# The opening of a fused recurrent-attention and expert kernel: who moves the first gate sums, who fills the head rows, and what stands ahead of the first units

## The chip, the cores and the metric

The kernel runs on one core of one Trainium2 chip. Its time is the device time of one execution in microseconds (us), the median of 3 runs. A row of the profile names five engines: PE (TensorE; PEld is its weight load), DVE (VectorE), ACT (ScalarE), POOL (GpSimd) and SP (SyncE). SP, ACT and POOL also issue transfers (DMA), which all share 16 DMA engines. A q behind an engine's name (SPq, ACTq) is its queue of issues.

## What is computed

An attention with exponential gates and a state, then a mixture of eight experts with the two best chosen for each token:

```python
batch, n_heads, seq, head_dim = (4, 8, 768, 40)
for t in range(S):
    m_new = np.maximum(f_gate[:, :, t] + m, i_gate[:, :, t])
    f_stab = np.exp(f_gate[:, :, t] + m - m_new)
    i_stab = np.exp(i_gate[:, :, t] - m_new)
    m = m_new
    C = f_stab[:, :, None, None] * C + i_stab[:, :, None, None] * np.einsum('bhd,bhe->bhde', vt, kt)
    n = f_stab[:, :, None] * n + i_stab[:, :, None] * kt
    h_tilde = np.einsum('bhde,bhe->bhd', C, qt)
    denom = np.maximum(np.abs(nq), 1.0)              # nq = n . q
    y[:, :, t] = o * h_tilde / denom                 # o = sigmoid(o_gate)
# x = y as 3072 tokens of 320
noisy_logits = x @ w_gate + np.log1p(np.exp(x @ w_noise)) * noise
# the two best of 8 experts; out += weight * (relu(x @ w1[e]) @ w2[e])
```

## The kernel before

The 768 steps of a sequence are cut into 12 chunks of 64, and two sequences are worked at a time (in the two halves of the partitions), so that the attention has 24 units. Unit u needs: its q and k (tile qk, four buffers, four loads: two of 32 partitions and two of 8), its k, v and output gate in rows (tile vk, four buffers, two loads), and a mask of 64 by 64 for every head, the exponential of a difference of gate sums. The masks come from PE: `e_part` multiplies LE by RE (98 rows) once for each sequence p, and ACT takes the exponential into W.

LE and RE exist twice, and each serves a group of two units: group 0 is units 0 and 1 (buffers le0, re0), group 1 is units 2 and 3 (le1, re1), group 2 is units 4 and 5 (le0, re0 again). They are put together of four pieces: constants copied by ACT (`operands`, L230), the head rows 64 to 95 of RE (`heads`, L237, 32 x 1024 for each p), and the gate sums of the group, which DVE works out in eight instructions (`gate_math`, L196, ending with L218) and which two small transfers then carry to other partitions (`gate_move`, L223: first le, then re). Before the masks of a group can be multiplied, all of these must be there.

Other work of the opening: `blank` clears qk where a load leaves gaps, and the 8-partition loads go on top of it; `keys` (L246, POOL: two memsets and two copies of a unit matrix from cs) prepares a vk buffer, which `k_part` (kd) and `c_part` read; `warm` runs dummy matmuls on PE. The third group's gate sums (256 to 383) are worked out by `gate_steps`, four instructions at a time.

The instructions of an engine run in the order in which the code is written. Order on PE at the start: 16 dummies, `s_part(0)` (scores), `WARM2` dummies, `e_part(0)`, `s_part(1)`, `e_part(1)`, then the loop over units. Pass i of the loop (L792) does `c_part(i)` (st, state), `o_part(i)` (o, output), the first half of the masks of unit i+2, later `s_part(i+2)`, then the other half of those masks. Behind the first half, ACT does the sigmoid of unit 0 in pass 0 (`sig_part`, L326 to L328), DVE normalises (`f_part`, L384 to L390), and POOL multiplies the two into xr (L391). In pass 0 POOL then issues `gate_move(2, (P, P))` (L840), the gate sums of group 2. The first half of unit 4's masks, in pass 2, reads them.

Transfers issued by SP and ACT raise one of eight counters, DMAHW0 to DMAHW7, taken in turn in the order of the code over both queues. A transfer that reuses a counter first waits until the transfer that had it before, eight places earlier, has landed; behind it in its queue everything waits too. POOL's transfers have eight counters of their own, DMASW0 to DMASW7.

After the attention come the routing (mostly within the loop) and eight experts of large matmuls.

Of the kernel before, what the change touches and what calls it, by code (L numbers as in the profile page):

```python
# [13 lines left out]
OP = mybir.AluOpType  # L14
# [4 lines left out]
L = 64  # L19
# [18 lines left out]
PAD = 544  # L38

STEP, SHARE = 0.19, 1.65  # L40
WARM, WARM2 = 16, 12
LEAD = 2
TURN = 6
OR1 = (0, 6, 1, 2, 3, 4, 5)
# [7 lines left out]
GC = 2  # L52
# [9 lines left out]
def build(ctx, tc, qk, vk, fi, noise, wgn, w1, w2, cst, ce, out):  # L62
    nc = tc.nc
    V, A, P, T, SP = nc.vector, nc.scalar, nc.gpsimd, nc.tensor, nc.sync
# [10 lines left out]
    cs = keep.tile([128, C_END], F32, name="cs")  # L75
# [78 lines left out]
    def load_unit(u, what="kv", q=None):  # L154
        pr, c = divmod(u, NCH)
        if "k" in what:
            for n in (slice(0, 32), slice(32, D)):
                for p in range(2):
                    (q or SP).dma_start(QK[u % 4][64 * p + n.start:64 * p + n.stop], qk[pr, c, p, n])
        if "v" in what:  # L160
            flat = VKS[u % 4].rearrange("p x c -> p (x c)")
            SP.dma_start(flat[0:64, 0:VW], vk[pr, c, 0])
            SP.dma_start(flat[64:128, 648:648 + VW], vk[pr, c, 1])
# [12 lines left out]
    def blank(i, q):  # L176
        q.memset(QK[i][32:64], 0.0)
        q.memset(QK[i][96:128], 0.0)
# [3 lines left out]
    V.memset(mt[:, 0:1], -1e30)  # L182
    blank(0, V)
    blank(1, P)
    V.memset(rmt[:, 0:256], 1.0)
    V.memset(rmt[:, 0:256].rearrange("p (c t) -> p c t", t=L)[:, :, 0], 0.0)
    load_unit(0, "k")
    SP.dma_start(cs[:, 0:128], cst[:, 0:128])
    SP.dma_start(fit[:, :, 128:384], fi[:, :, 128:384])
    load_unit(0, "v")  # L190

    def run(steps):
        for _ in steps:
            pass

    def gate_math(t0, t1):  # L196
        f, i = fit[:, 0, t0:t1], fit[:, 1, t0:t1]
        n = t1 - t0
        V.tensor_tensor_scan(mt[:, t0 + 1:t1 + 1], f, i, mt[:, t0:t0 + 1], OP.add, OP.max)
        yield  # L200
        gt = gts[t0 // 128 % 2][:, 0:n]
        V.tensor_add(gt, f, mt[:, t0:t1])
        yield
        V.tensor_sub(gt, gt, mt[:, t0 + 1:t1 + 1])
        if t0 == 0:
            V.memset(gt[:, 0:1], 0.0)
        yield
        ag = ags[t0 // 128 % 2][:, :, 0:n]
        V.tensor_tensor_scan(ag[:, 1, :], rmt[:, 0:n], gt, 0.0, OP.mult, OP.add)
        yield  # L210
        V.tensor_sub(ag[:, 0, :], i, mt[:, t0 + 1:t1 + 1])
        yield
        V.tensor_sub(ag[:, 0, :], ag[:, 0, :], ag[:, 1, :])
        yield

        V.tensor_copy(HL[:, :, t0:t1], ag)
        yield
        V.scalar_tensor_tensor(HL[:, :, t0:t1], HL[:, :, t0:t1].bitcast(F32), cet[0:64, E_SG:E_SG + 1], ag, op0=OP.mult, op1=OP.add)  # L218
        yield
# [3 lines left out]
    def gate_move(kk, q=(SP, SP)):  # L223
        pr, k = divmod(kk, GB)
        j = kk % 2
        src = HL[32 * pr:32 * pr + 32, :, k * GC * L:(k + 1) * GC * L].bitcast(F32)
        q[0].dma_start(LE[j][64:96, :, 64:128].bitcast(F32), src[:, 0].rearrange("r (c t) -> r c t", c=GC))
        q[1].dma_start(RE[j][96:98].bitcast(F32), src[:, 1])

    def operands(j, p, eng=None):  # L230
        if p is None:
            A.activation(LE[j][0:KE], cet[0:KE, None, E_L:E_L + 192].to_broadcast([KE, GC, 192]), AF.Copy)
        else:
            A.activation(RE[j][0:64, p].rearrange("r h (c t) -> r h c t", c=GC),
                         cet[0:64, None, None, 0:L].to_broadcast([64, H, GC, L]), AF.Copy)

    def heads(j, p, eng):  # L237
        o, i = RE[j][64:96, p], cet[64:96, E_H:E_H + H, None].to_broadcast([32, H, GC * L])
        x = cet[64:96, E_P + p:E_P + p + 1]
        if eng is A:  # L240
            A.activation(o, i, AF.Copy, scale=x)
        else:
            V.tensor_scalar(o, i, x, None, op0=OP.mult)


    def keys(i):  # L246
        P.memset(VK[i][1][32:64, 0:328], 0.0)
        P.memset(VK[i][0][96:128, 328:648], 0.0)
        P.tensor_copy(VK[i][0][64:104, 328:648].rearrange("p (h d) -> p h d", h=H), ident[64:104, None, 64:104].to_broadcast([40, H, D]))
        P.tensor_copy(VK[i][1][0:64, 328:648].rearrange("p (h d) -> p h d", h=H), ident[0:64, None, 0:D].to_broadcast([64, H, D]))  # L250

    operands(0, None, A)
    load_unit(1, "k", A)
    run(gate_math(0, GC * L))
    gate_move(0)
    operands(0, 0, A)
    operands(0, 1, A)
    heads(0, 0, A)
    heads(0, 1, A)
    load_unit(1, "v")  # L260
    blank(2, P)
    for i in range(2):
        keys(i)
    load_unit(2, "k")
    operands(1, None, A)
    operands(1, 0, A)
    run(gate_math(GC * L, 256))
    gate_move(1)
    heads(1, 0, V)
    gates2 = (s for t0 in (256, 384, 512, 640) for s in gate_math(t0, t0 + 128))  # L270

    def gate_steps(n):
        for _ in range(n):
            next(gates2, None)

    gate_steps(4)
    blank(3, P)
    for i in range(2, 4):
        keys(i)
    load_unit(2, "v")  # L280
    load_unit(3, "k")
    SP.dma_start(fit[:, :, 384:], fi[:, :, 384:])
# [61 lines left out]
    def whole(u):  # L344
        return u % NCH > 0

    def k_part(u):
        if u % NCH < NCH - 1:
            KD[u] = wk.tile([128, 2, H, D], F32, name="kd")
            V.tensor_mul(KD[u], VKS[u % 4][:, :, 328:648].rearrange("p x (h d) -> p x h d", h=H),  # L350
                         W[u][:, :, :, L - 1:L].to_broadcast([128, 2, H, D]))

    def p_part(u):
        PP[u] = wk.tile([128, 2, H, L], F32, name="p")
        if whole(u):
            V.tensor_mul(PP[u], SQ[u], W[u])
        else:
            for p in range(2):
                n = half[p]
                V.tensor_mul(PP[u][n, p], SQ[u][n, p], W[u][n, p])  # L360
# [336 lines left out]
    warm(WARM2)  # L697
    e_part(0, first=True)
    s_part(1)
    heads(1, 1, A)  # L700
    e_part(1, first=True)
    operands(1, 1, A)
    k_part(0)
    p_part(0)

    load_unit(3, "v")
    def route(i):
# [83 lines left out]
    i = 0  # L791
    while i < NU - LEAD:  # L792
        unit[0] = i
        spent[0] = 0.0
        while sent:
            SP.dma_start(*sent.pop())
        if 1 <= i and i + 3 < NU:
            load_unit(i + 3)
        if i:
            keep_rows(i - 1)  # L800
        if i % 2 == 0 and i and i // 2 + 2 < 2 * GB:
            gate_move(i // 2 + 2, (P, P) if i < XV else (SP, SP))

        if W1LD <= i < W1LD + 12 and i % 2 == 0:
            j = (i - W1LD) // 2
            piece_w1(0, 512 * (j // 3), j % 3)
        if i == W2AT:
            early_w2(0, 2)
        if i == 3:
            SP.dma_start(cs[:, C_TRI:], cst[:, C_TRI:])  # L810
        if i == 4:
            SP.dma_start(nzt, noise)
        if not begun and done[0] >= E0U[0]:
            decode(0, E0S[1] // 128)
            spent[0] += 0.6
            begun = 1
        if begun and late < len(tiles(0, 0)):
            gather(0, 0, tiles(0, 0)[late:late + 2])
            late += 2
            begun = 2  # L820
        if i == 6:
            constants()
            A.activation(tri, cs[:, C_TRI:C_TRI + 128], AF.Copy)
            A.activation(ones, cs[:, C_ONE:C_ONE + 128], AF.Copy)
            A.activation(iob, cs[:, C_N:C_N + 128], AF.Copy)
        k_part(i + 1)
        p_part(i + 1)
        fill(0.2, False)
        s_room(i + 2)
        c_part(i)  # L830
        o_room(i)
        o_part(i)
        e_part(i + LEAD, (0,))
        if i == 0:
            sig_part(0)
        f_part(i, lambda: fill(0.15, False))
        if i < 2:
            gate_steps(4)
        if i == 0:
            gate_move(2, (P, P))  # L840
        t = l_part(i)
        w = r_part(t)
        b = None if w else b_part(t)
        if i:
            t_part(i - 1)
            tc_part(i - 1)
        lc_part(i, t, w)
        bc_part(t, b)
        s_part(i + 2)
        act()  # L850
        if i:
            sig_part(i + 1)
        e_part(i + LEAD, (1,))
        if i == 0:
            sig_part(1)
        route(i)
        fill((SHARE if i < NU - 3 else 0.8) - spent[0])
        if W1AT <= i < W1AT + 12 and i % 2 == 0:
            next(pre1)
        act()  # L860
        if 0 < i < 7:
            gate_steps(4)
        if 6 <= i < 13:
            P.memset(XG[:, i - 6], 0.0)
        i += 1
# [352 lines left out]
    with tc.If(over > 0):  # L1218
        for i in range(NE):
            n = BLK - CAPS[i]  # L1220
            more = nc.values_load(flag[0:1, 2 + i:3 + i], min_val=0, max_val=16 * NTOK)
            with tc.If(more > 0):
# [4 lines left out]
                x = xf[0:n, 0:RW]  # L1227
# [12 lines left out]
        with tc.If(most > BLK):  # L1240
            V.memset(ec, 0.0)
            with tc.For_i(0, NE, 1) as e:
                weights(e)
                with tc.For_i(0, NCH, 1) as c:
# [8 lines left out]
                    for r in range(2):  # L1253
                        x = xf[:, DM * r:DM * r + DM]
# [93 lines left out]
```

## Time and profile before

| | us |
|---|---|
| median of 3 runs (lowest to highest) | 523.07 (521.63 to 526.06) |
| the profiled execution | 522.65 |
| its span, first to last instruction | 520.9 |
| PE busy in the span | 504.6 (97%) |
| DVE, ACT, POOL busy | 341.3, 248.7, 243.3 |
| first mask on PE begins | 12.20 |
| first half of unit 4's masks begins | 29.00 |

The profiled execution lies 0.42 us under the median, and its span 1.75 us under its own time. Matmuls are pipelined, so a busy PE isn't PE at its peak. The chain of waits is followed back from the last instruction: it names at each step what released the step. A wait for several things is put down to the one that came last by the profile.

### The profile page before, as it was taken

The page shows a single profiled execution, that of the slowest core. Times are in us where ns is not written, and L with a number is a line of the kernel's source. Part 1 is how long each engine was busy: PE and PEld are TensorE (multiplying, and loading weights), DVE is VectorE, ACT ScalarE, POOL GpSimd, SP SyncE. Part 2 cuts the span into 40 slices and gives each one's busy share as a digit, 9 for nine tenths or more (in the row PEclk, how much of TensorE's full clock was granted, in tenths as well). Part 3 has the DMA queues.
Part 4 walks back from the last instruction along what each step waited for, and adds up shares of the span by engine and source line. Part 5 has one row for each costly group of instructions (what it writes and reads, how often), then busy time and mean ns, then how long its engine had stood idle before and what let it go on. Part 6 is the DMA issues. An engine that isn't in the chain of part 4 may idle for free.

```text
span 520.9 us, 13365 instructions
## 1 busy us (share of the span) xinstructions
PE 504.6 (97%) x5130; PEld 473.3 (91%) x5130; DVE 341.3 (66%) x905; ACT 248.7 (48%) x594; POOL 243.3 (47%) x321
## 2 busy tenths in 40 slices
PE   8899999999999999999999999999999999999993
PEld 3788888888889988999999999999999999999993
DVE  6899998986997576763865484377548347546310
ACT  5788879978523255441542354054335325515300
POOL 7545686864543846055415614550562254151033
PEclk9799999999989999999999999999999999999998
DMA  5889999986655848079229516832951683272033
GB/s 153 201 217 243 246 242 248 223 235 207 216 195 165 202 57 213 5 163 234 68 53 274 112 28 139 229 91 48 263 99 51 138 221 88 60 169 26 2 40 41
DMA packets 48955, 76.89 MB, mean 148 GB/s; under 512 B 10645, under 2 KB 37980, under 8 KB 48884
## 3 DMA queue, kind: packets, MB, share of 16 engines
q1 hardware_dynamic: 35668, 52.19, 36.3%
q0 software_dynamic: 11616, 20.57, 20.7%
q10 hardware_dynamic: 1600, 3.21, 2.0%
q8 instruction: 42, 0.69, 0.6%
q14 instruction: 29, 0.24, 0.2%
HBM read 52.42 MB, written 17.40 MB: 134 GB/s over the span
## 4 chain that ended last, share of the span: by engine, by line
PE 66%; DMA 13%; DVE 11%; ACT 3%; issue 2%; POOL 2%; SPq 1%; POOLq 0%; DVEq 0%; ACTq 0%
PE s L981 16%; DMA y_out<-y,tok 9%; PE e L981 8%; PE o L1009 4%; PE o L1008 4%; PE o L1007 4%; PE st L1008 4%; PE st L1009 4%; PE st L1007 4%; PE o L379 4%; PE e L318 3%; PE s L342 2%; DVE hlo L993 2%; PE st L370 2%; DMA qk<-qk_in 2%
## 5 line engine op out<-in xcount | busy, mean ns | idle before, releaser
L1035 POOL DMA_INDIRECT y_out<-y,tok x53 | 87.2, 1645 | 184.8 <-DVE y L1025 182.0
L992 ACT ACTIVATE hh<-s 128x384 fp32r<-128x384 f32 (+3 forms) x91 | 42.6, 470 | 83.8 <-PE s L981 82.7
L981 PE MATMUL s<-xh,w1h 128*128 128x384 f32 (+6 forms) x273 | 76.8, 337 | 0.1
L750 POOL DMA_INDIRECT xg<-rows,tok x53 | 57.3, 1082 | 24.6 <-issue 15.5
L993 DVE SCALAR_TENSOR_TENSOR hlo<-s,hh 128x384 fp32r<-128x384 f32 (+3 forms) x91 | 47.6, 523 | 24.9 <-ACT hh L992 24.3
L981 PE MATMUL s<-xh,w1l 128*128 128x384 f32 (+6 forms) x273 | 61.7, 334 | 0.0
L1009 PE MATMUL o<-w2h,hlo 128*128 128x320 f32 x184 | 56.9, 309 | 0.7 <-DVE hlo L993 0.7
L1008 PE MATMUL o<-w2l,hh 128*128 128x320 f32 x184 | 56.8, 309 | 0.0
L1007 PE MATMUL o<-w2h,hh 128*128 128x320 f32 x184 | 56.3, 306 | 0.2 <-ACT hh L992 0.2
L1009 PE MATMUL st<-w2h,hlo 128*128 128x320 f32 x168 | 51.9, 309 | 0.0
L1008 PE MATMUL st<-w2l,hh 128*128 128x320 f32 x168 | 51.8, 308 | 0.0
L1007 PE MATMUL st<-w2h,hh 128*128 128x320 f32 x168 | 51.2, 305 | 0.0
L981 PEld LDWEIGHTS s<-xh,w1h 128*128 128x128 f32 x273 | 49.2, 188 | 1.5 <-ACT xh L782 0.4
L981 PEld LDWEIGHTS s<-xh,w1l 128*128 128x128 f32 x273 | 47.7, 188 | 1.1 <-DVE xh L784 0.2
L981 PE MATMUL s<-xl,w1h 128*128 128x384 f32 (+6 forms) x182 | 46.1, 334 | 0.3 <-DVE xl L783 0.3
L992 ACT ACTIVATE hh<-e 128x384 fp32r<-128x384 f32 (+3 forms) x45 | 21.3, 473 | 49.3 <-PE e L981 49.3
L981 PE MATMUL e<-xh,w1h 128*128 128x384 f32 (+6 forms) x135 | 38.6, 340 | 0.6 <-DVE hlo L993 0.3
L1025 DVE TENSOR_SCALAR y<-o,gw 128x320 f32<-128x320 f32 x22 | 12.1, 550 | 39.9 <-PE o L1009 39.9
L391 POOL TENSOR_TENSOR xr<-tm,vk 128x320 f32<-128x320 f32 x24 | 21.1, 879 | 34.7 <-DVE tm L390 13.6
L1025 DVE TENSOR_SCALAR y<-st,gw 128x320 f32<-128x320 f32 x20 | 11.0, 550 | 39.3 <-PE st L1009 39.3
L1009 PEld LDWEIGHTS o<-w2h,hlo 128*128 128x128 f32 x184 | 34.5, 188 | 0.9 <-DVE hlo L993 0.9
L1007 PEld LDWEIGHTS o<-w2h,hh 128*128 128x128 f32 x184 | 34.5, 188 | 0.6 <-ACT hh L992 0.4
(237 smaller groups left out, 1290.7 us busy)
## 6 DMA issues: line engine op xcount, KB each, us to landing
vk<-vk_in SPq DMA_DIRECT2D x48, 242.0 KB
raw<-w_in SPq DMA_DIRECT2D x6, 1280.0 KB
raw<-w_in SPq DMA_DIRECT2D x6, 1024.0 KB
qk<-qk_in SPq DMA_DIRECT2D x46, 128.0 KB
y_out<-zrow SPq DMA_DIRECT2D x15, 320.0 KB
raw<-w_in SPq DMA_DIRECT2D x16, 256.0 KB
rows<-xr POOLq DMA_DIRECT2D x23, 160.0 KB, 4.3
xt__2801<-xb SPq DMA_DIRECT2D x40, 72.0 KB
```

Of the source, the lines that this page charges most:

```text
L318: T.matmul(ps, LE[j][0:KE, c, 64 - 64 * p:192 - 64 * p], RE[j][0:KE, p, :, c * L:c * L + L], start=True, stop=True)
L379: T.matmul(OQ[u][half[p], h, :], PP[u][n, p, h, :], VK[u % 4][p][n, h * 41:h * 41 + 41], start=True, stop=True)
L391: P.tensor_mul(XR[u], tm.rearrange("p h d -> p (h d)"), SG[u % 4])
L750: P.indirect_dma_start(out=XG[0:rows_of(e, t), t], out_offset=None, in_=XD[0:n], in_offset=bass.IndirectOffsetOnAxis(ap=token(e, t), axis= ...
L981: T.matmul(ps[:, 0:n], l, r, start=i == 0, stop=i == len(ops) - 1)
L992: A.activation(hi, x, AF.Relu)
L993: V.scalar_tensor_tensor(lo, x, 0.0, hi.bitcast(F32), op0=OP.max, op1=OP.subtract)
L1007: T.matmul(ps, HH[:, j, c], W2H[:, j], start=j == 0, stop=False)
L1008: T.matmul(ps, HH[:, j, c], W2L[:, j], start=False, stop=False)
L1009: T.matmul(ps, HLO[:, j, c], W2H[:, j], start=False, stop=j == 7)
L1025: V.tensor_scalar(y[0:n], ps[0:n], GW[e][0:n, t:t + 1], None, op0=OP.mult)
L1035: st = P.indirect_dma_start(out=out, out_offset=bass.IndirectOffsetOnAxis(ap=token(e, t), axis=0), in_=y[0:n], in_offset=None, compute_op= ...
```

## The change

- The second set of dummies has 6 instead of 12.
- SP loads the unit matrix (cs) ahead of unit 0's q and k, and unit 1's q and k, which ACT issued, are now issued by SP behind unit 0's vk.
- The gate sums of group 0 are issued by ACT instead of SP.
- The head rows: (0,0) go from ACT to POOL, (0,1) from ACT to DVE, (1,0) from DVE to POOL, (1,1) from ACT to POOL.
- The first four instructions of the third group's gate arithmetic go from ahead of the first units' DVE work to behind `p_part(0)`.
- On POOL `blank(2)` is written earlier, and `keys(3)` goes from ahead of the loop into pass 0, between xr of unit 0 and `gate_move(2)`.

```diff
@@ -38,7 +38,7 @@
 PAD = 544
 
 STEP, SHARE = 0.19, 1.65
-WARM, WARM2 = 16, 12
+WARM, WARM2 = 16, 6
 LEAD = 2
 TURN = 6
 OR1 = (0, 6, 1, 2, 3, 4, 5)
@@ -182,12 +182,14 @@
     V.memset(mt[:, 0:1], -1e30)
     blank(0, V)
     blank(1, P)
+    blank(2, P)
     V.memset(rmt[:, 0:256], 1.0)
     V.memset(rmt[:, 0:256].rearrange("p (c t) -> p c t", t=L)[:, :, 0], 0.0)
+    SP.dma_start(cs[:, 0:128], cst[:, 0:128])
     load_unit(0, "k")
-    SP.dma_start(cs[:, 0:128], cst[:, 0:128])
     SP.dma_start(fit[:, :, 128:384], fi[:, :, 128:384])
     load_unit(0, "v")
+    load_unit(1, "k")
 
     def run(steps):
         for _ in steps:
@@ -240,7 +242,7 @@
         if eng is A:
             A.activation(o, i, AF.Copy, scale=x)
         else:
-            V.tensor_scalar(o, i, x, None, op0=OP.mult)
+            eng.tensor_scalar(o, i, x, None, op0=OP.mult)
 
 
     def keys(i):
@@ -250,33 +252,30 @@
         P.tensor_copy(VK[i][1][0:64, 328:648].rearrange("p (h d) -> p h d", h=H), ident[0:64, None, 0:D].to_broadcast([64, H, D]))
 
     operands(0, None, A)
-    load_unit(1, "k", A)
-    run(gate_math(0, GC * L))
-    gate_move(0)
     operands(0, 0, A)
     operands(0, 1, A)
-    heads(0, 0, A)
-    heads(0, 1, A)
+    heads(0, 0, P)
+    keys(0)
+    run(gate_math(0, GC * L))
+    gate_move(0, (A, A))
+    heads(0, 1, V)
     load_unit(1, "v")
-    blank(2, P)
-    for i in range(2):
-        keys(i)
+    keys(1)
     load_unit(2, "k")
     operands(1, None, A)
     operands(1, 0, A)
     run(gate_math(GC * L, 256))
     gate_move(1)
-    heads(1, 0, V)
+    heads(1, 0, P)
+    heads(1, 1, P)
     gates2 = (s for t0 in (256, 384, 512, 640) for s in gate_math(t0, t0 + 128))
 
     def gate_steps(n):
         for _ in range(n):
             next(gates2, None)
 
-    gate_steps(4)
     blank(3, P)
-    for i in range(2, 4):
-        keys(i)
+    keys(2)
     load_unit(2, "v")
     load_unit(3, "k")
     SP.dma_start(fit[:, :, 384:], fi[:, :, 384:])
@@ -697,11 +696,11 @@
     warm(WARM2)
     e_part(0, first=True)
     s_part(1)
-    heads(1, 1, A)
     e_part(1, first=True)
     operands(1, 1, A)
     k_part(0)
     p_part(0)
+    gate_steps(4)
 
     load_unit(3, "v")
     def route(i):
@@ -837,6 +836,7 @@
         if i < 2:
             gate_steps(4)
         if i == 0:
+            keys(3)
             gate_move(2, (P, P))
         t = l_part(i)
         w = r_part(t)
```

The built programs differ on each engine up to pass 0 alone; behind it the order is the same. Three places follow, with the waits of each row. In the names the number behind qk, vk, le and re is the buffer (unit 0 to 3 for qk and vk, group 0 or 1 for le and re); hl is the tile that holds the gate sums.

SP before, from unit 0's vk on:

```order
L162 DMA vk0_104<-vk_in 64x968 [waits DMAHW4_49]
L163 DMA vk0_104<-vk_in 64x968 [waits DMAHW5_49]
L227 DMA le0_94<-hl_96 32x2x64 [waits DMAHW6_49,DVE_49,Activation_49]
L228 DMA re0_92<-hl_96 2x16x128 [waits DMAHW7_49]
L162 DMA vk1_105<-vk_in 64x968 [waits DMAHW0_49]
L163 DMA vk1_105<-vk_in 64x968 [waits DMAHW1_49]
L159 DMA qk2_102<-qk_in 32x1024 [waits DMAHW2_49]
L159 DMA qk2_102<-qk_in 32x1024 [waits DMAHW3_49]
L159 DMA qk2_102<-qk_in 8x1024 [waits DMAHW4_49,Pool_49]
L159 DMA qk2_102<-qk_in 8x1024 [waits DMAHW5_49,Pool_49]
L227 DMA le1_95<-hl_96 32x2x64 [waits DMAHW6_49,DVE_49,Activation_49]
L228 DMA re1_93<-hl_96 2x16x128 [waits DMAHW7_49]
```

SP now, from behind unit 0's vk on:

```order
L159 DMA qk1_101<-qk_in 32x1024 [waits DMAHW4_49]
L159 DMA qk1_101<-qk_in 32x1024 [waits DMAHW5_49]
L159 DMA qk1_101<-qk_in 8x1024 [waits DMAHW6_49,Pool_49]
L159 DMA qk1_101<-qk_in 8x1024 [waits DMAHW7_49,Pool_49]
L162 DMA vk1_105<-vk_in 64x968 [waits DMAHW0_49]
L163 DMA vk1_105<-vk_in 64x968 [waits DMAHW1_49]
L159 DMA qk2_102<-qk_in 32x1024 [waits DMAHW2_49]
L159 DMA qk2_102<-qk_in 32x1024 [waits DMAHW3_49]
L159 DMA qk2_102<-qk_in 8x1024 [waits DMAHW4_49,Pool_49]
L159 DMA qk2_102<-qk_in 8x1024 [waits DMAHW5_49,Pool_49]
L229 DMA le1_95<-hl_96 32x2x64 [waits DMAHW6_49,DVE_49,Activation_49]
L230 DMA re1_93<-hl_96 2x16x128 [waits DMAHW7_49]
```

The two issues for le0 and re0 are gone from SP, and four for qk1 stand there. le0 and re0, now on ACT, take the counters DMAHW6 and DMAHW0, as PE's wait for the first mask shows; so qk1's third piece waits on SP for le0 to land, and vk1's first for re0. PE now, from the first mask on:

```order
L317 MATMUL e_260<-re0_92,le0_94 128x512 [waits DMAHW0_49,DMAHW6_49,Activation_49,Pool_49]
L317 MATMUL xt_205<-re0_92,le0_94 128x512 [waits DVE_49,Activation_49]
L338 MATMUL s_236<-qk1_101,cs_66 64x256 [waits DMAHW7_49,DMAHW5_49,DMAHW2_49]
L338 MATMUL s_236<-qk1_101,cs_66 64x256 [waits DMAHW6_49,DMAHW4_49]
L341 MATMUL s_236<-qk1_101 64x64 x8
L338 MATMUL s_236<-qk1_101,cs_66 64x256 x2
L341 MATMUL s_236<-qk1_101 64x64 x8
L317 MATMUL e_286<-re0_92,le0_94 128x512 [waits Activation_49]
```

The first mask now waits for POOL too, its other half for DVE, and `s_part(1)` (L338) for all four pieces of qk1.

POOL near the start, before:

```order
L177 MEMSET qk2_102 32x1024
L178 MEMSET qk2_102 32x1024
L247 MEMSET vk0_104 32x328
L248 MEMSET vk0_104 32x320
L249 COPY vk0_104<-cs_66 40x320 [waits DMAHW1_49,Pool_49]
L250 COPY vk0_104<-cs_66 64x320
L247 MEMSET vk1_105 32x328 [waits Pool_49]
L248 MEMSET vk1_105 32x320
L249 COPY vk1_105<-cs_66 40x320 [waits Pool_49]
L250 COPY vk1_105<-cs_66 64x320
```

and now (ISA is an instruction that names the library of POOL's code, L245 the head rows):

```order
L177 MEMSET qk2_102 32x1024
L178 MEMSET qk2_102 32x1024
L245 ISA
L245 TENSOR_SCALAR re0_92<-raw1_115 32x1024 [waits DMAHW1_49]
L249 MEMSET vk0_104 32x328
L250 MEMSET vk0_104 32x320
L251 COPY vk0_104<-cs_66 40x320 [waits DMAHW2_49,Pool_49]
L252 COPY vk0_104<-cs_66 64x320
L249 MEMSET vk1_105 32x328 [waits Pool_49]
L250 MEMSET vk1_105 32x320
L251 COPY vk1_105<-cs_66 40x320 [waits Pool_49]
L252 COPY vk1_105<-cs_66 64x320
```

The head rows of (0,0), with the ISA instruction ahead of them, now stand ahead of all four `keys(0)` instructions; behind `keys(1)` come the two others for group 1. POOL at the end of the opening, before:

```order
L481 MEMSET anew_8_219 128x72
L482 MEMSET anew_8_219 128x8 [waits Pool_49]
L391 ISA
L391 TENSOR_TENSOR xr_365<-tm_366,vk0_104 128x320 [waits DMAHW4_49,DMAHW5_49,DVE_49,Activation_49]
L227 DMA le0_94<-hl_96 32x2x64 [waits DMAHW6_49,DVE_49,PE_49]
L228 DMA re0_92<-hl_96 2x16x128 [waits DMAHW7_49]
L394 DMA rows_65<-xr_365 128x320 [waits Pool_49]
```

and now:

```order
L480 MEMSET anew_8_212 128x72
L481 MEMSET anew_8_212 128x8 [waits Pool_49]
L390 TENSOR_TENSOR xr_355<-tm_356,vk0_104 128x320 [waits DMAHW2_49,DMAHW3_49,DVE_49,Activation_49]
L249 MEMSET vk3_107 32x328 [waits Pool_49]
L250 MEMSET vk3_107 32x320
L251 COPY vk3_107<-cs_66 40x320 [waits Pool_49]
L252 COPY vk3_107<-cs_66 64x320
L229 DMA le0_94<-hl_96 32x2x64 [waits DMAHW6_49,DVE_49,PE_49]
L230 DMA re0_92<-hl_96 2x16x128 [waits DMAHW0_49]
L393 DMA rows_65<-xr_355 128x320
```

The ISA instruction is gone from here, and the four of `keys(3)` stand between xr and the two issues for le0 and re0 of group 2.

## Rows read from the trace of the kernel before

**Rows 1.** Chain of waits, 0 to 30 us: start, us, what.
```profile
4.23 2.98 DMA qk<-qk_in
...
8.49 0.71 SPq L227
...
9.24 2.82 DMA re<-hl
...
12.20 0.48 PE e L318
...
17.36 1.92 PE o L379 x30
19.29 0.72 PE e L318
...
25.04 0.43 PE e L318
...
29.00 0.42 PE e L318
```

**Rows 2.** Timeline of DVE: start, us, instruction, count, idle time before it.
```profile
6.46 0.47 DVE L218 SCALAR_TENSOR_TENSOR hl<-hl,raw,xg 64x256 fp32r<-64x256 f32 x1
...
15.19 0.79 DVE L350 TENSOR_TENSOR kd<-vk,w 128x640 f32<-128x640 f32 x1
```

**Rows 3.** Timeline of ACT.
```profile
6.24 2.00 ACT L234 ACTIVATE re<-raw 64x1024 fp32r<-64x1024 f32 x2 [1.49 <-DMA qk<-qk_in]
...
13.20 0.59 ACT L321 ACTIVATE w<-xt 128x512 f32<-128x512 f32 x1
...
20.05 0.60 ACT L321 ACTIVATE w<-e 128x512 f32<-128x512 f32 x1 [1.98 <-PE e L318]
...
21.54 0.47 ACT L328 ACTIVATE vk<-vk 128x320 f32<-128x320 f32 x1
```

**Rows 4.** Timeline of PE without its weight loads.
```profile
8.76 2.76 PE L691 MATMUL o<-wz 128*128 128x512 bf16 x12
...
12.83 0.43 PE L339 MATMUL s<-qk,cs 64*64 64x256 f32 x2
```

**Rows 5.** Timeline of SP's issues.
```profile
9.24 0.74 SPq L228 DMA_DIRECT2D re<-hl  x1
...
11.25 1.81 SPq L159 DMA_DIRECT2D qk<-qk_in  x4
...
13.89 0.70 SPq L228 DMA_DIRECT2D re<-hl  x1
```

**Rows 6.** Timeline of POOL.
```profile
3.73 0.95 POOL L178 MEMSET qk<- 32x1024 f32 x1
...
7.31 0.45 POOL L249 COPY vk<-cs 40x320 f32<-40x320 f32 x1 [1.82 <-DMA cs<-cst_in]
...
8.30 0.36 POOL L247 MEMSET vk<- 32x328 f32 x1
...
17.44 0.13 POOL L482 MEMSET anew<- 128x8 bf16 x1
22.09 0.86 POOL L391 TENSOR_TENSOR xr<-tm,vk 128x320 f32<-128x320 f32 x1 [4.52 <-DMA raw<-fi_in]
...
23.68 0.69 POOL L228 DMA_DIRECT2D re<-hl  x1
```

**Rows 7.** POOL's instructions by line and shape: busy us, mean ns | idle before.
```profile
L151 POOL TENSOR_TENSOR w1l<-raw,w1h 128x512 fp32r<-128x512 f32 x4 | 6.2, 1544 | 1.9 <-ACT w1h L150 1.9
```

**Rows 8.** Issue to landing: POOL's first re (0 to 30 us), and all re.
```profile
re<-hl POOLq DMA_DIRECT2D x1, 16.0 KB, 4.5
...
DMA to landing us min/median/max: 4.5/4.9/6.6
```

**Rows 9.** Stretches: length, busy us (instructions) by engine, granted TensorE clock, DMA share, GB/s.
```profile
18.00:20.00 2.00, 2.00 (x29) 1.49 (x25) 1.90 (x5) 0.07 (x1) 0.00 (x0) 0.50 0.90 246
...
40.00:70.00 30.00, 30.00 (x751) 26.19 (x750) 27.31 (x76) 26.55 (x69) 19.79 (x35) 1.00 0.97 248
```

## The prediction

> **What bounds the opening now.** I read the chain of waits first, since a change to the first 30 us can only pay where that chain passes. It shows one line of cause: SP's queue stands until a load of unit 1's qk, issued by ACT at 4.23, has landed 2.98 later, because SP's next load reuses its counter; then SP issues le0 at 8.49 and re0 at 9.24, re0 lands at 12.06, and the first mask starts at 12.20 [rows 1]. The timelines of the engines say who was early. DVE had the gate sums ready at 6.46 + 0.47 = 6.93, 1.56 before SP issued them [rows 2]. The masks of unit 0 were exponentiated at 13.20 + 0.59 = 13.79, but DVE began kd at 15.19 only, the third group's gate arithmetic being ahead of it [rows 2, 3]. From 17.36 on the chain is PE alone: unit 0's output part, unit 2's first masks at 19.29, unit 3's at 25.04, unit 4's at 29.00 [rows 1]. Part of that ran at 1.2 GHz: the granted clock is 0.50 in 18 to 20 us; the stretch from 19.29 to 25.04 took 5.75, the like one behind it at the high clock 3.96 [rows 1, 9]. Later, from 40 to 70 us, PE is busy for all of 30.00 us and the DMA engines for 0.97 of it [rows 9]. So PE paces the loop, and what the opening gains goes into the time if nothing between takes it back. The search is for what is late next.
>
> **First mask.** ACT no longer issues qk1; its two RE fills waited 1.49 for that, and end at 8.24 - 1.49 = 6.75 instead of 8.24 [rows 3]. So ACT can issue le0 at 6.97, right behind the gate sums, and re0 0.75 later at 7.72, which is 1.52 earlier than before. With the same 2.82 to landing, re0 is there at 10.54. Before, two vk loads stood ahead of it in the same queue; ACT's own qk load took 2.98 in traffic [rows 1]: 10.5 to 10.7. Twelve dummies took 2.76, so 0.23 each; six end at 8.76 + 1.38 = 10.14 [rows 4], so they delay nothing, and twelve would have held the mask until 11.52.
>
> The head rows (0,0) are new on POOL. They can start at 3.73 + 0.95 = 4.68. POOL's copy of 320 took 0.45, so 1024 come to 1.44; a memset of 1024 took 0.95, which is the lower end; the two-operand w1l at 512 took 1.544, so 3.09 is the upper [rows 6, 7]. I take 1.4, as this too streams one operand: ready at 6.1, far ahead of 10.54. DVE has 3.6 us for (0,1) behind 6.93. W of unit 0 is then ready at 10.54 + (13.79 - 12.20) = 12.1, and kd no longer queues behind gate arithmetic.
>
> **Scores of unit 1.** Here a wait is added. SP may issue qk1's third piece only once le0 has landed, at 6.97 + 2.82 = 9.79. Behind it on SP wait its fourth piece, vk1, qk2, le1 and re1. Four such issues took 1.81, so the fourth piece is issued at 10.24 and lands at about 13.06: `s_part(1)` starts at 13.1 against 12.83 [rows 1, 4, 5]. The 1.5 us at the first mask are gone at this point. But the rest follows faster, for DVE is no longer late: 3.96 of PE work for a whole unit [rows 1] puts the end of `o_part(0)` at 17.0 or earlier, against 19.28.
>
> **Masks of unit 2** need re1. Between re0's issue, over at 9.98, and re1's at 13.89 lay seven issues, 3.91 us [rows 5]; now they start at 10.69, so re1 goes out at 14.60 and lands 2.82 later, at 17.42. Unit 2's masks start there, 1.87 earlier than at 19.29.
>
> **Masks of unit 4** need group 2's gate sums, moved by POOL, and this is where I look hardest. Before: masks 19.29, exponential 20.05, end of the sigmoid 21.54 + 0.47 = 22.01, xr 22.09 (its row names a DMA, but that instruction waits for the sigmoid too, which ended 0.08 earlier), re0 issued at 23.68, landed 4.5 later at 28.2, mask at 29.00: only 0.8 to spare [rows 1, 3, 6, 8]. Now: 17.42 + 0.76 + 1.96 + 0.08 = 20.22 for xr; then `keys(3)` in between, two memsets of 0.36, two copies of 0.45 and their gaps, 1.75 [rows 6]; then 1.59 as before to re0's issue at 23.56; landing at 28.06 with 4.5 and at 28.46 with the median of 4.9 [rows 8]. PE would be ready at 29.00 - 1.87 = 27.1. So the moved `keys(3)` gives most of the gain back: 0.94 or 0.54 stay of 1.87. I take 0.7. Ten landings ranged from 4.5 to 6.6, so the lower end of the gain is below zero.
>
> **POOL's queue up to xr.** Before it was through at 17.44 + 0.13 = 17.57. Now three head rows come in (4.2), the wait of 1.82 for cs falls away (cs now goes ahead of unit 0's q and k), `keys(3)` leaves (1.75): 18.2, with 2.0 to spare before 20.22. That holds if head rows cost 1.4 and the ISA instruction nothing. The ISA instruction stood in the idle 4.52 before xr; there the sigmoid ended the wait, so its cost was hidden, anything from 0 to 4.5 [rows 6]. Its cover is gone: ahead of the first head rows nothing hides it. I take near 0, because the 0.86 of the instruction behind it and its start 0.08 after the sigmoid show no trace of a load, but keep 4.5 for the range.
>
> The Trainium skill (GPSIMD Engine Reference, Instruction dispatch) says that the first call behind a freshly loaded library pays about 6 us, measured 5.95, which no row shows. The 4.52 before xr can't hold 5.95, so this trace contradicts the figure, though not a smaller one; by the page the first mask would wait for POOL until 4.68 + 5.95 + 1.4 = 12.0, and unit 4's masks would come about 3 us later than before.
>
> **Sum.** First mask -1.52, unit 2 -1.87, unit 4 -0.7, and that remains. The other edits (the cs load, `blank(2)`, third-group arithmetic) are worth nothing of their own: they free DVE and POOL ahead of points where PE now waits for transfers. Against the profiled execution's 522.65, 0.42 under the median: 522.0.
>
> **Rivals.**
> - *The gain carries.* If the POOL transfer lands a microsecond sooner, unit 4's masks start at 27.1, and the time is 522.65 - 1.87 = 520.8. For it: PE is ready. Against: 4.5 was the least of all ten landings. 0.12.
> - *POOL becomes the bound (slower).* Place: POOL's queue up to xr. Point: over 2.0 of extra work delays xr, over 2.9 makes the kernel slower. An ISA of 4.5 makes xr 2.5 late, net +1.6, 524.2; head rows at 3.09 each add 5.1, so 3.1 late, net +2.2, 524.8; both, 7.6 late, net +6.7, 529.3. For it: an ISA instruction does stand there, and both prices are taken near their lower ends. Against: before, xr started right behind its last input. 0.26.
> - *The clock.* PE stands for about a microsecond before unit 4's masks, and before unit 1's scores. If a unit more runs at 1.2 GHz, that is 5.75 - 3.96 = 1.8 dearer: 523.8. 0.12. If instead the early low stretch disappears, nothing is gained, since unit 4's masks come no sooner.
>
> **Numbers.** The forecast has 0.50: 521.5 to 522.9 on its own. The range, 520.4 to 525.2, takes in the first rival in part, either price on POOL alone, and the clock. A measurement of this kernel tells about 1% (5.2 us) from no change; only both POOL prices together reach that, and no case gives 5 us of gain: faster 0.03, same 0.91, slower 0.06.
>
> **What would show it.** Right: le0 issued by ACT near 7.0, first mask near 10.5, `s_part(1)` near 13 with PE idle before it, unit 2's masks near 17.4, xr near 20.2 released by ACT, unit 4's masks at 28 to 28.5 released by POOL's re. Wrong: xr released by POOL's own queue, a gap of microseconds ahead of the first head rows, or masks of unit 4 that PE reaches late by itself.

## The result: 0.8% slower, and the profile after

The changed kernel takes 527.53 us (median of 21 runs, 523.43 to 533.2), the one before 522.96 (21 runs, 519.93 to 529.32). The ratio is 1.0077, 95% interval 1.0055 to 1.0099: about 4.0 us slower. That lies inside the 1% that the prediction called no change, but outside its range, which ended at 525.2, and on the other side of its forecast of 522.0. Ratios and intervals leave out executions more than 1.5% above the fastest of their kernel, and medians don't, so a ratio is not quite the quotient of two medians.

| | before | after |
|---|---|---|
| profiled execution, us | 522.65 | 528.76 |
| its span, us | 520.9 | 526.9 |
| its mean granted clock | 0.985 | 0.973 |
| first mask, us | 12.20 | 11.98 |
| unit 2's masks | 19.29 | 18.65 |
| unit 4's masks | 29.00 | 30.61 |
| unit 6's masks | 38.65 | 45.76 |

The timeline of POOL after (start, us, instruction, count) answers to [rows 6]:

```profile
3.73 0.95 POOL L178 MEMSET qk<- 32x1024 f32 x1
4.78 2.98 POOL L245 TENSOR_SCALAR re<-raw 32x1024 fp32r<-32x1024 f32 x1
...
12.03 5.77 POOL L245 TENSOR_SCALAR re<-raw 32x1024 fp32r<-32x1024 f32 x2
...
22.28 0.13 POOL L481 MEMSET anew<- 128x8 bf16 x1
22.47 0.87 POOL L390 TENSOR_TENSOR xr<-tm,vk 128x320 f32<-128x320 f32 x1
23.39 0.36 POOL L249 MEMSET vk<- 32x328 f32 x1
...
24.74 0.45 POOL L252 COPY vk<-cs 64x320 f32<-64x320 f32 x1
25.13 0.80 POOL L229 DMA_DIRECT2D le<-hl  x1
25.94 0.68 POOL L230 DMA_DIRECT2D re<-hl  x1
```

Three things are to be seen. A head row takes 2.98 us here, and the two at 12.03 take 5.77 together. POOL has no idle time left ahead of xr: its queue is through at 22.41 and xr starts 0.06 later, where it stood 4.52 idle before [rows 6]. And between xr and the two issues lie the four instructions of `keys(3)`, 1.8 us.

The chain of waits after, 25 to 46 us, answers to the last lines of [rows 1]:

```profile
25.94 4.54 DMA re<-hl
30.61 0.47 PE e L317
...
38.33 0.73 PE e L317
...
45.76 0.43 PE e L317
```

The lines at 30.61, 38.33 and 45.76 are the first masks of units 4, 5 and 6. Before, the chain gave 29.00 for unit 4 and for the next two:

```profile
34.07 0.43 PE e L318
...
38.65 0.43 PE e L318
```

So unit 4 starts 1.61 late, and units 4 and 5 then take 15.15 us where they took 9.65. The timeline of PE puts the wait at 1.91, and the stretches (length, busy us by engine, granted clock, DMA share, GB/s) show the clock behind it, at 0.57 and 0.58 where it was 1.00 before:

```profile
30.61 0.47 PE L317 MATMUL e<-re,le 98*128 98x512 f32 x1 [1.91 <-DMA re<-hl]
```
```profile
30.00:38.00 8.00, 7.39 (x113) 6.50 (x115) 6.58 (x12) 3.94 (x9) 2.71 (x4) 0.57 0.90 246
38.00:46.00 8.00, 8.00 (x124) 6.88 (x121) 4.55 (x9) 3.93 (x9) 2.63 (x4) 0.58 0.80 208
```

At unit 6 this execution is 7.1 us behind; at its end 6.0. So its loss is made by then, and the work behind it only takes some back. The median is 4.6 behind, so one profile may not be taken for all executions; a second one stands below.

### The profile page after: what moved, and what is told of

Same layout as the page of the kernel before. It is cut to its first block, busy times and chain, and to the rows that moved or that the text cites. A ratio compares the mean times of both kernels' runs of the same rounds, so it can differ in the third digit from the quotient of the medians.

```text
span 526.9 us, 13355 instructions
## 1 busy us (share of the span) xinstructions
PE 508.0 (96%) x5124; PEld 476.0 (90%) x5124; DVE 343.2 (65%) x905; ACT 245.2 (47%) x591; POOL 251.7 (48%) x324
## 3 DMA queue, kind: packets, MB, share of 16 engines
q10 hardware_dynamic: 1586, 2.92, 1.7%
## 4 chain that ended last, share of the span: by engine, by line
PE 62%; DMA 13%; DVE 11%; POOL 6%; ACT 3%; issue 2%; SPq 1%; POOLq 0%; DVEq 0%; ACTq 0%
PE s L981 15%; DMA y_out<-y,tok 9%; PE e L981 8%; PE o L1009 4%; PE o L1008 4%; PE o L1007 4%; PE st L1009 4%; PE st L1008 4%; PE st L1007 4%; PE o L378 3%; DVE hlo L993 3%; PE e L317 2%; PE s L341 2%; PE st L369 2%; PE xt L421 2%
```

## The experiments

Theory A: POOL's queue, lengthened by two parts of the change (three head rows ahead of xr, `keys(3)` behind it, between xr and the move of group 2's gate sums), brings group 2's gate sums late, and unit 4's masks with them. Rivals: one of the two parts alone, the slower clock behind PE's wait, or what is left of the change (ACT's issues, SP's loads, six dummies). Intervals are 95%; the time of before is that of runs on the same chip beside them.

| label | kernel | us | before | ratio | interval |
|---|---|---|---|---|---|
| e10_after_again | changed, again | 526.16 | 522.40 | 1.0075 | 1.0042 to 1.0108 |
| e1_heads_back | without head rows on POOL | 526.12 | 522.72 | 1.0049 | 1.0011 to 1.0086 |
| e2_keys_behind | keys(3) behind the move | 523.19 | 522.72 | 1.0012 | 0.9979 to 1.0045 |
| e2b_keys_behind | the same, again | 523.40 | 522.22 | 1.0021 | 0.9991 to 1.0052 |
| e3_heads_keys | both | 521.88 | 522.22 | 0.9988 | 0.9957 to 1.0018 |
| e6_before_keys3 | before, keys(3) moved alone | 526.06 | 522.22 | 1.0049 | 1.0015 to 1.0083 |
| e4_before_pool_heads | before, head rows alone | 527.00 | 522.72 | 1.0093 | 1.0057 to 1.0130 |
| e5_dummies | changed, dummies in the wait | 526.39 | 522.72 | 1.0058 | 1.0017 to 1.0099 |
| e8_after_sp_move | changed, move by SP | 524.21 | 522.40 | 1.0044 | 1.0012 to 1.0075 |
| e9_heads_keys_sp | both, move by SP | 522.28 | 522.40 | 1.0009 | 0.9979 to 1.0040 |
| e7_heads_keys_12 | both, 12 dummies | 523.91 | 522.22 | 1.0021 | 0.9992 to 1.0050 |
| e11_qk_first | both, qk1 ahead of vk0 | 523.13 | 521.52 | 1.0010 | 0.9979 to 1.0042 |

**The changed kernel again.**

> The changed kernel itself once more, on the chip of these runs, for a profile of another execution: whether the slow stretch of 13.65 us behind unit 4's masks belongs to the kernel or to that one execution. If it belongs to the kernel, units 4 and 5 run at 1.2 GHz again and take about 15 us together, where 9.65 were needed before; if not, they take 10 to 12 us, and the time is still 525 to 528.

Its chain and its PE timeline, around unit 4:

```profile
26.45 4.69 DMA re<-hl
31.27 0.77 PE e L317
...
43.59 0.43 PE e L317
```
```profile
31.27 0.77 PE L317 MATMUL e<-re,le 98*128 98x512 f32 x1 [3.66 <-DMA re<-hl]
```
```profile
30.00:38.00 8.00, 6.73 (x115) 5.83 (x115) 4.88 (x11) 3.84 (x9) 2.62 (x4) 0.61 1.01 256
```

PE was ready at 27.6 in this execution, earlier than in the first, and the masks still came at 31.27. So their time is set by POOL's transfer, not by PE. The slow stretch is there again (0.61) but shorter: units 4 and 5 take 12.32. The delay belongs to the kernel, the length of the slow stretch to the execution. This one is 4.9 behind at unit 6's masks (43.59 against 38.65) and 3.2 at its end (a span of 524.1 against 520.9): here too the loss is made in the opening, and not later.

**Head rows off POOL, the rest as changed.**

```diff
-    heads(0, 0, P)
     keys(0)
     run(gate_math(0, GC * L))
     gate_move(0, (A, A))
+    heads(0, 0, A)
     heads(0, 1, V)
...
-    heads(1, 0, P)
-    heads(1, 1, P)
+    heads(1, 0, V)
...
     s_part(1)
+    heads(1, 1, A)
```

> The changed kernel with the three head rows taken off POOL again: (0,0) on ACT behind its two issues, (1,0) on DVE, (1,1) on ACT behind the scores of unit 1; all other edits stay, keys(3) ahead of the gate sums' move too. Theory A, POOL's queue: the head rows took 2.98 + 5.77 us of POOL, xr started at 22.47 right behind POOL's own work and unit 4's masks came at 30.61 in place of 29.00. Then POOL is idle ahead of xr here, xr starts at 20.2 to 21.5 released by ACT, unit 4's masks come at 28.1 to 29.5, and the time is 521 to 524. Gate sums should be ready at 6.9 instead of 8.43 (DVE is no longer held while POOL works on head rows), and the first mask near 10.5. Rival B, the move of keys(3) alone is what costs: masks of unit 4 still past 30, time 526 to 528. Rival C, the opening is not the cause and the loss is later: 526 to 528 with the masks early.

```profile
21.07 0.87 POOL L389 TENSOR_TENSOR xr<-tm,vk 128x320 f32<-128x320 f32 x1 [7.19 <-DVE hl L220]
...
24.73 0.69 POOL L230 DMA_DIRECT2D re<-hl  x1
```
```profile
10.93 0.47 PE L316 MATMUL e<-re,le 98*128 98x512 f32 x1 [0.67 <-DMA re<-hl]
13.02 0.52 PE L337 MATMUL s<-qk,cs 64*64 64x256 f32 x2 [1.39 <-DMA qk<-qk_in]
```

These are its POOL and its PE timeline. POOL is idle for 7.19 ahead of xr, and xr comes 1.40 earlier than in the changed kernel; the first mask comes at 10.93, near the 10.5 foreseen. The time did not follow as theory A put it (521 to 524): 526.12. `keys(3)` still stands ahead of the issues and holds re0 to 24.73, against 23.68 before [rows 6]. The time is rival B's. Its masks are not: in this execution PE reached unit 4's by itself at 29.90, after a long stretch at the low clock:

```profile
14.00:22.00 8.00, 8.00 (x135) 6.17 (x130) 6.61 (x15) 5.42 (x11) 0.87 (x2) 0.50 0.83 198
22.00:30.00 8.00, 8.00 (x168) 7.01 (x164) 7.01 (x15) 6.29 (x14) 5.49 (x10) 0.64 0.92 226
```

So this profile hides what `keys(3)` costs, and the interval of the time is wide. The next two runs decide.

**keys(3) behind the two issues.**

```diff
-            keys(3)
             gate_move(2, (P, P))
+            keys(3)
```

> The changed kernel with one line moved: keys(3) stands behind the two issues that move group 2's gate sums, not ahead of them. The head rows stay on POOL. xr should stay at 22.47; the issues come 1.78 us earlier (le0 at 23.35, re0 at 24.15), re0 lands near 28.7, when PE has just ended unit 2's output part (28.70), so PE hardly stands. Theory A with the clock (PE's pause of 1.91 us is followed by two units at 1.2 GHz, 15.15 us from unit 4's masks to unit 6's where 9.65 were needed before): the pause goes and with it the slow stretch, 1.8 + up to 5.5 less, so 520.5 to 523. Without the clock, by the delay alone: 1.8 less, 525.5 to 526.

> e2_keys_behind once more, for a closer interval and a profile of another execution: median 522.5 to 524 as there (523.2), against 527.5 of the changed kernel; masks of unit 4 near 29.2, and less time at 1.2 GHz between 30 and 46 us than the 13.65 us that the changed kernel's profile has.

The median falls to 523.19 and 523.40, for one line moved. The chain of the second run (the first one's profile is of an execution of 534.10, 11 us above its median):

```profile
22.49 0.88 POOL xr L390
...
24.12 4.82 DMA re<-hl
29.08 0.47 PE e L317
```

xr stays where the head rows put it, re0 is issued 1.82 earlier, and unit 4's masks come at 29.08, as before. PE was ready at 27.2 here and still stands 1.9, and a stretch at the low clock follows (0.79 in 30 to 38), yet the masks of unit 6 come at 39.74 in its chain, 1.1 behind before. So the place of `keys(3)` is worth about 0.6% (1.0077 less 1.0012 to 1.0021), some 3 us. By their intervals this difference is known to about 0.4%, so it is more than noise, but the 1.8 us of the delay alone (0.34%) are not excluded.

**Both undone.** The two diffs above together.

> The changed kernel with both parts undone: head rows off POOL as in e1_heads_back, and keys(3) behind the two issues as in e2_keys_behind. What is left of the change: ACT moves the first gate sums, SP takes unit 1's q and k, blank(2) and cs early, the third group's gate arithmetic behind the first masks, six dummies. Theory A, POOL's queue ahead of group 2's transfer is the cause, both parts on it: first mask 10.9 as in e1_heads_back, xr near 21, le0 issued right behind it near 22.0, re0 lands near 27.5, PE reaches unit 4's masks by itself at 28 to 29.5; time 521 to 523.5. Rival B, what is left loses by itself (PE stood 1.4 us ahead of unit 1's scores in e1_heads_back, and 13.65 us at 1.2 GHz followed): 525 to 527, as e1_heads_back.

521.88: no difference from before (1.0 within 0.9957 to 1.0018). Theory A's time holds, rival B's of 525 to 527 doesn't. Its timelines:

```profile
20.99 1.13 POOL L389 TENSOR_TENSOR xr<-tm,vk 128x320 f32<-128x320 f32 x1 [7.12 <-ACT vk L326]
22.14 0.78 POOL L229 DMA_DIRECT2D le<-hl  x1
22.93 0.69 POOL L230 DMA_DIRECT2D re<-hl  x1
```
```profile
27.45 0.47 PE L316 MATMUL e<-re,le 98*128 98x512 f32 x1 [1.06 <-ACT vk L371]
```

Unit 4's masks at 27.45 no longer wait for POOL's re. One way from the changed kernel back to before goes by these runs: head rows 0.28% (changed, less the run without them), `keys(3)` 0.61% (from the run without head rows to this one), what is left -0.12%. In us these are about 1.5, 3.2 and -0.6. They come to the 4.0 that were lost, as they must, each run being subtracted from the next. What tests the sizes is another way: `keys(3)` 0.56 to 0.65% in the pair above and 0.49% alone on before, head rows 0.24 to 0.33% (`keys(3)` behind, with and without them). The head rows' own share and what is left are below what the intervals of these ratios can tell from nothing.

**Each part alone on before.** `keys(3)` between xr and the move:

> The kernel before with one part of the change alone: keys(3) leaves its place ahead of the loop and stands between xr and the move of group 2's gate sums. Head rows, loads and dummies as before. xr stays at 22.1 (POOL stood 4.52 idle ahead of it), le0 and re0 are issued 1.75 later (re0 near 25.4), re0 lands near 30, and as the slack was 0.8, unit 4's masks come about 0.95 late, near 29.9. Theory A by the delay alone: 1.0 slower, 523.5 to 524.5. With a slow stretch behind PE's pause of 1 us: 526 to 528. Rival: hidden, 522 to 523.

526.06, 0.49% (0.15 to 0.83) slower, that is 0.8 to 4.3 us: slower than before, but the interval holds both the 1.0 us by the delay alone and the 3 us of the pair above. Its profile is of its slowest execution (529.64), and the first mask of unit 4 comes 0.82 late there, behind a wait for re, as expected:

```profile
29.82 0.47 PE L317 MATMUL e<-re,le 98*128 98x512 f32 x1 [1.40 <-DMA re<-hl]
```

The three head rows on POOL:

> The kernel before with one part of the change alone: the three head rows (0,0), (1,0), (1,1) on POOL. keys(3) stays ahead of the loop, the loads as before. If a head row costs 2.9 us on POOL as in the changed kernel, 8.7 us go into a queue that had 4.52 idle before xr: xr starts about 4.2 late, near 26.3, re0 is issued near 27.9 and lands near 32.4, so unit 4's masks come 3.4 late and PE stands for over 3 us; time 3.4 over before, and 526 to 532 with a slow stretch behind the pause. If the head rows are not the cause (they cost 1.4 as forecast, or are hidden): 522 to 524.

527.00, 0.93% slower, as theory A had it. But its wait is another one:

```profile
22.35 2.84 POOL L243 TENSOR_SCALAR re<-raw 32x1024 fp32r<-32x1024 f32 x1
```
```profile
25.24 0.79 PE L318 MATMUL e<-re,le 98*128 98x512 f32 x1 [6.24 <-POOL re L243]
```

In the order of before, row (1,1) comes last in POOL's queue, and unit 2's second masks wait 6.24 for that row itself. So this run shows what a head row costs on POOL (2.84 to 2.92), not the changed kernel's wait.

**Dummies in PE's wait.**

```diff
+            for _ in range(8 if u == 4 and p == 0 else 0):
+                T.matmul(ps, wz[:, 0:128], wz, start=True, stop=True)
             T.matmul(ps, LE[j][0:KE, c, ...
```

> The changed kernel with eight dummy matmuls on PE ahead of unit 4's first mask, 0.23 us each, so 1.84 in the pause of 1.91 in which PE waits for POOL's re. Nothing else moves: the masks of unit 4 still come near 30.6. Theory, the clock: PE does not stand, the granted clock stays at 1.00 from 30 to 46 us, unit 6's masks come near 40.4 instead of 45.76, and the time falls by up to 5.4, to 522 to 524. Rival, the lateness itself costs and the clock is made good later in the loop: 527 to 528, as the changed kernel.

```profile
29.23 1.90 PE L318 MATMUL e<-wz 128*128 128x512 bf16 x7
30.78 0.59 PE L319 MATMUL e<-re,le 98*128 98x512 f32 x1
```
```profile
30.00:38.00 8.00, 8.00 (x172) 6.67 (x169) 7.58 (x16) 5.45 (x14) 2.72 (x4) 1.00 0.85 236
```

The lateness is the same, the slow stretch behind it is gone, and this execution took 524.23. But the median of twelve is 526.39, which can't be told from the changed kernel. So the clock accounts for the 5.5 us of one profile, and that it accounts for the loss over all executions is not shown. Two further numbers speak against it. The changed kernel's executions at a mean granted clock of 0.986 or more took 522.1 to 529.1, those at 0.979 or less 523.4 to 529.5 (and one 533.2). This mean counts a low stretch wherever it lies, and an early one need not cost anything: the profile of e9_heads_keys_sp (below) has one from 14 to 22 us, and its span is 519.9, 1.0 under before:

```profile
14.00:22.00 8.00, 8.00 (x136) 6.47 (x128) 6.74 (x15) 5.08 (x10) 0.18 (x1) 0.50 0.83 194
```

And with the two parts undone and twelve dummies as before,

> e3_heads_keys with the twelve dummies of before in place of six. First mask 11.5 instead of 10.9 if dummies of 0.23 us hold it; PE stands less between the scores of unit 0 and the first mask. If PE's pauses ahead of unit 1's scores start the slow stretch, the dummies change little there, and the time is within 1 us of e3_heads_keys; if the pause ahead of the first mask does, the granted clock falls later than 14 us and the time is 1 to 2 us less than e3_heads_keys.

the profile has the full clock from 0 to 140 us, and the median is 523.91, not less than with six dummies:

```profile
0.00:140.00 140.00, 129.56 (x2784) 107.92 (x2786) 119.72 (x328) 108.83 (x258) 86.42 (x145) 1.00 0.84 217
```
```profile
18.40 0.47 PE L316 MATMUL e<-re,le 98*128 98x512 f32 x1 [1.86 <-DMA re<-hl]
```

At the full clock PE stood for data instead, here 1.86 for unit 2's re.

**The move on another queue.**

```diff
-            gate_move(2, (P, P))
+            gate_move(2, (SP, SP))
```

> The changed kernel with one thing moved: group 2's gate sums go by SP's queue, not POOL's. POOL does all that it did, head rows and keys(3) ahead. Theory A (what costs is that the transfer stands behind POOL's work): SP is through with unit 3's v near 22.5, issues le0 and re0 there, and re0 lands 2.8 later as other loads of SP's queue did, near 27; PE reaches unit 4's masks by itself near 28.7 to 29.2; the time falls by 2 to 4, to 523 to 525. Rival: POOL's late xr or the early part costs, not the transfer: 526.5 to 528 as the changed kernel. Against a gain speaks that two issues of 0.75 each now stand ahead of unit 4's q and k on SP.

```profile
27.38 0.50 PE L317 MATMUL e<-re,le 98*128 98x512 f32 x1
...
30.79 0.52 PE L338 MATMUL s<-qk,cs 64*64 64x256 f32 x2 [1.96 <-DMA qk<-qk_in]
```

POOL does all its work, xr comes late as in the changed kernel (22.50), and unit 4's masks no longer wait: 27.38. The time falls by 0.3% to 524.21, in the range expected, though the two intervals overlap. Part of the gain goes where the expectation said: unit 4's q and k now stand behind the two issues on SP, and PE waits 1.96 for them. With head rows and `keys(3)` undone as well:

> e3_heads_keys (head rows off POOL, keys(3) behind) with group 2's gate sums moved by SP too, as a candidate for the fastest. In e3_heads_keys PE stood 1.1 us ahead of a mask for re; if that goes, 1 less than e3_heads_keys: 520.5 to 522. If unit 4's q and k come late behind the two issues on SP: 522 to 524.

522.28, no better than without. Last, the loads in another order:

```diff
+    load_unit(1, "k")
     SP.dma_start(fit[:, :, 128:384], fi[:, :, 128:384])
     load_unit(0, "v")
-    load_unit(1, "k")
```

> e3_heads_keys with SP's loads in another order: unit 1's q and k ahead of the second piece of f and i and of unit 0's v. In e3_heads_keys qk1's third piece stood on SP until le0 had landed, and PE stood 1.4 us for it ahead of unit 1's scores. Now no piece of qk1 reuses the counter of le0. If the loss of the first mask's gain lies there, s_part(1) starts 1 to 1.4 earlier (near 12), and the time is 1 less than e3_heads_keys: 520 to 521.5. If it is handed on to the next transfer (unit 0's v or unit 2's masks), the time stays at 521.5 to 523.

The scores of unit 1 start at 11.27 instead of 13.10, and the gain is handed on: unit 2's masks come at 18.45, against 18.35 without it. No version was measurably faster than before.

## Why the prediction was wrong, step by step

**Head rows at 1.4 each: the first step that failed.** They took 2.98 and twice 2.84 to 2.85; the upper bound of 3.09 [rows 7] was nearly right, the copy of 320 from which 1.4 was scaled was not. The two differ in form: a head row multiplies by a value per partition and writes fp32r (as the w1l rows of [rows 7] do), and the copy does neither. Which of the two costs, no run tells apart. With 8.7 in the place of 4.2, the forecast 18.2 for POOL's queue becomes 22.7, against 22.41 measured; the 2.0 to spare were gone. This step alone doesn't make the miss: with the head rows off POOL (e1_heads_back) re0 was still issued at 24.73, not at 23.56, and the kernel was still 0.49% slower.

**The rival "POOL becomes the bound"** named this place, this price and the later masks: net +2.2, and +1.6 with the 8.7 that were measured (4.5 more work, 2.0 to spare, 0.9 of gain), against +1.61. What it lacked is what follows late masks: it counted a microsecond of lateness as a microsecond of time, and the loss was 4.0.

**keys(3) between xr and the issues: the second step that failed, in what was to pay for it.** It was priced right at 1.75 (1.79 measured) and then set off against 1.87 gained upstream. The gain at unit 2's masks was 0.64, and 0.94 with both parts undone; in the changed kernel nothing of it reached xr, which stood behind POOL's queue. So most of the lateness against before is this term: xr itself came only 0.38 later than before (22.47 against 22.09).

**First mask at 10.54.** It came at 11.98. ACT's queue was free as foreseen, but the gate sums were ready at 8.43 (7.95 + 0.48), not 6.93. DVE's timeline, against [rows 2], says why; the prediction had not asked what POOL's new work does to DVE:

```profile
5.19 1.10 DVE L211 TENSOR_TENSOR_SCAN xg<-raw,xg 64x128 f32<-64x128 f32 x1
6.21 0.26 DVE L213 TENSOR_TENSOR xg<-raw,xg 64x128 f32<-64x128 f32 x1
6.50 0.28 DVE L215 TENSOR_TENSOR xg<-xg 64x128 f32<-64x128 f32 x1
6.82 1.09 DVE L218 CAST hl<-xg 64x256 fp32r<-64x256 f32 x1
7.95 0.48 DVE L220 SCALAR_TENSOR_TENSOR hl<-hl,raw,xg 64x256 fp32r<-64x256 f32 x1
```

The same scan and cast with the head rows off POOL took 0.42 and 0.46, and there the first mask came at 10.93. From the end of the gate sums to the mask it took 3.55 here and 3.69 there (where they were ready at 7.24), so what moved the mask is the gate sums:

```profile
5.18 0.42 DVE L211 TENSOR_TENSOR_SCAN xg<-raw,xg 64x128 f32<-64x128 f32 x1
...
6.27 0.46 DVE L218 CAST hl<-xg 64x256 fp32r<-64x256 f32 x1
```

**Scores of unit 1 at 13.1** held: 12.96. **Unit 2's masks at 17.42** did not: 18.65, and 18.35 even with both parts undone. SP's queue is the reason; it issued re1 at 15.57, not at 14.60:

```profile
6.08 5.17 SPq L159 DMA_DIRECT2D qk<-qk_in  x4
11.75 0.48 SPq L162 DMA_DIRECT2D vk<-vk_in  x1
...
14.80 0.72 SPq L229 DMA_DIRECT2D le<-hl  x1
15.57 0.75 SPq L230 DMA_DIRECT2D re<-hl  x1
```

The four pieces of qk1 took 5.17 to issue, with a stand up to 10.60 ahead of the third, and the queue was through with them at 11.25, not at 10.69. Then vk1's first piece stood until 11.75; it waits for re0 to land, which at the prediction's 10.54 would have cost nothing. So the opening's gain was 0.6 at this point, not 1.87.

**The ISA instruction at about 0** held: the head row started 0.10 behind the last memset of `blank(2)`, as the second of the two later head rows did behind the first (0.09), with no ISA instruction between them. The sentence of the Trainium skill on it (GPSIMD Engine Reference, Instruction dispatch: about 6 us at the first call behind a freshly loaded library) is not borne out here.

**The gain carries, 520.8.** The runs with both parts undone made its condition true: unit 4's masks at 27.45, 1.5 earlier than before. They took 521.88, 0.1% less than before, with an interval of both signs. So even without its fault the change was worth less than this kernel's measurement can tell.

**The clock** was a rival by itself, at 0.12. In the two profiles it came with the POOL rival: late masks made PE stand, and with its stands of 1.91 and of 3.66 came a stretch at 1.2 GHz each. The two should have been one case with one chance; with two units dearer by the prediction's 1.8 each, its 524.8 becomes 528.4.

**Open:** why masks that came 1.61 and 2.27 late in two profiles cost some 4 us over all executions. The clock does it in these two; dummies that took it away in a third did not bring the median down. In all profiles but that of e2_keys_behind, what an execution is behind before (or ahead of it) at unit 6's masks changes by at most 1.7 us up to its end (2.2 in e7_heads_keys_12), so the first 46 us are the place to search. Nothing here shows what the executions that have no profile waited for.

## What to carry to other kernels

Before moving work onto an engine that also issues transfers, price it by a row of the same form (operands, output type), and where only a range is known, let the dear end decide whether the queue keeps its slack. Put work that nobody waits for behind an issue that somebody waits for: one line's place was worth 0.6% here. Rivals that start each other are one case, and the range must hold them together.

## What the hardware showed

- The same instruction, 32x1024 fp32 to fp32r by a value per partition, took 743 ns on DVE and 2836 to 2985 on POOL. The view of tile re, with ns as least, median and most, then first and last start:

```profile
L245 POOL TENSOR_SCALAR re<-raw x3: 2836/2839/2985, 4.8 to 15.0; 32x1024 fp32r<-32x1024 f32 x3
L245 DVE TENSOR_SCALAR re<-raw x1: 743/743/743, 8.5 to 8.5; 32x1024 fp32r<-32x1024 f32 x1
```

- While POOL ran it (4.78 to 7.76), a cast on DVE took 1.09, ending 0.15 after POOL, and a scan 1.10. The Trainium skill (SBUF — State Buffer, the notes to its diagram of ports) says that POOL and some DVE instructions, those in a two-port mode and, against a POOL instruction that reads SBUF, those with two inputs, share a pair of ports as a lock, which the first to start keeps for its whole instruction. The cast agrees. The scan ended 1.5 before POOL did, and two subtractions of two inputs between them took their usual 0.26 and 0.28; so for those the trace does not bear the sentence out.
